# Sliding-window attention followed by an MLP: batching the softmax normalisation per head, and writing the attention loop as a software pipeline

## Chip, core and metric

The kernel runs on one core of a Trainium2 chip. The metric is the device time of one execution in microseconds (us). The kernel before took 407.39 us when it was first measured (median of 6 runs, 407.08 to 408.81).

## The reference

Four batches, eight heads, 768 positions, head size 64. A query sees the first 8 positions and the last 96 up to its own, with a distance bias that differs by head. The attention output, reshaped to 3072 x 512, goes through a two-layer MLP with a squared ReLU.

```python
scores = (1.0 / np.sqrt(D)) * np.matmul(q, k.transpose(0, 1, 3, 2))
keep = is_global | is_local                  # pos < 8, or 0 <= rel < 96
scores = np.where(keep, scores + bias, -1000000000.0)
a = np.exp(scores - np.max(scores, axis=-1, keepdims=True))
a = a / (np.sum(a, axis=-1, keepdims=True) + 1e-09)
x = np.matmul(a, v)                          # to (B*S, H*D)
h = x @ w_in                                 # 512 -> 2048
out = np.maximum(h, 0.0) ** 2 @ w_out        # 2048 -> 512
```

## The kernel before

Two heads form a pair; there are 16 pairs. For each pair, q and k of both heads are loaded, transposed on TensorE (12 transposes; the result lies in PSUM, as all matmul results of this kernel do) and copied by VectorE to SBUF, where its other tiles lie. Each head then has six tiles of 128 queries. A tile multiplies one to three blocks of keys with the queries (contraction over the 64 elements of a head), ScalarE takes the exponential, VectorE multiplies with a table of mask and bias, and TensorE multiplies with V. V has a 65th column of ones, so the row sum comes out beside the output, and VectorE divides by it.

```python
for b in range(B):
    for kp in range(H // 2):
        # ... load q_b, k_b; 12 transposes into qT_ps, kT_ps ...
        nc.vector.tensor_copy(qT2, qT_ps)
        nc.vector.tensor_copy(kT2, kT_ps)
        for hh in range(2):
            # ... load vS, then set its column of ones ...
            for t in range(N_ROW_TILES):
                # ... 1 to 3 score matmuls into sc_ps: lhsT = keys, rhs = queries, 64 rows each ...
                nc.scalar.activation(out=esc[:, :ncols], in_=sc_ps[:, :ncols], func=Act.Exp, scale=scale)
                nc.vector.tensor_mul(attnT[:, :ncols], esc[:, :ncols], expBT[h][cfg])
                out_ps = psum_out.tile([128, D + 1], FP32, tag="out_ps")
                # ... 1 to 3 output matmuls into out_ps ...
                nc.vector.reciprocal(rsum, out_ps[:, D : D + 1])
                nc.vector.tensor_scalar(out=x_sbuf[:, b * N_ROW_TILES + t, h, :], in0=out_ps[:, :D],
                                        scalar1=rsum, scalar2=None, op0=mybir.AluOpType.mult)
```

The program is not run in the order of this text: a scheduler places the instructions on each engine's queue when the kernel is built. The traces show the matmuls in the order that was built: the built order of this kernel changes 22 times per pair between scores and other matmuls, and so does its trace.

The softmax here doesn't subtract the row's maximum and nothing guards it: scores larger than these inputs give would overflow.

## Time and profile before

| Part of the span | Time |
|---|---|
| to the first score matmul (constants, MLP weights, first q and k) | 34.1 us |
| attention, 16 pairs, first score to last output | 180.7 us |
| rest: MLP | about 192 us |
| period of a head pair in the steady state | 11.35 us |

The first line is the busy time of each engine from the page; the second is one row of the windows view, 50 us of steady attention (busy us and instruction count of PE, of its weight loads PEld, of DVE, ACT and POOL, then granted TensorE clock, DMA share, GB/s); the third is the first long MLP piece in the chain of waits (start, duration).

```profile
PE 331.7 (81%) x2016; PEld 165.2 (41%) x2016; DVE 199.6 (49%) x712; ACT 161.2 (40%) x361; POOL 89.3 (22%) x158
...
50.00:100.00 50.00, 42.29 (x322) 24.72 (x320) 33.94 (x168) 22.28 (x53) 24.00 (x37) 1.00 0.84 54
...
216.62 4.85 PE hT_ps L290 x11
```

The clock of 1.00 in the second line is not a measurement: the trace has no clock record before 222.3 us, and the view prints 1.00 where there is none.

No engine is busy all the time in attention: TensorE (PE) has work for 42.3 of 50 us and VectorE (DVE) for 33.9. The next lines, the timeline of PE around the end of a pair, show where the rest goes (start, duration, what; in brackets the idle time and what ended it).

```profile
86.09 0.50 PE L218 MATMUL sc_ps<-qT,kT 64*128 64x128 bf16 x3
86.52 0.35 PE L239 MATMUL out_ps<-vS,attnT 128*128 128x65 bf16 x3
86.80 0.29 PE L218 MATMUL sc_ps<-qT,kT 64*128 64x128 bf16 x1
87.25 0.24 PE L239 MATMUL out_ps<-vS,attnT 128*128 128x65 bf16 x1 [0.17 <-DVE attnT L235]
87.42 0.39 PE L218 MATMUL sc_ps<-qT,kT 64*128 64x128 bf16 x2
87.94 0.29 PE L239 MATMUL out_ps<-vS,attnT 128*128 128x65 bf16 x2
88.40 0.70 PE L239 MATMUL out_ps<-vS,attnT 128*128 128x65 bf16 x6 [0.17 <-DVE attnT L235]
89.62 0.35 PE L239 MATMUL out_ps<-vS,attnT 128*128 128x65 bf16 x3 [0.52 <-DVE attnT L235]
90.49 0.35 PE L239 MATMUL out_ps<-vS,attnT 128*128 128x65 bf16 x3 [0.52 <-DVE attnT L235]
91.14 0.60 PE L218 MATMUL sc_ps<-qT,kT 64*128 64x128 bf16 x4 [0.31 <-DVE kT L189]
```

From 87.9 to 91.1 us TensorE has only output matmuls to do (14 of them), and all groups but the first show a wait for VectorE's mask multiply (attnT). It could not run the scores of the next pair, because the copy of the next keys (kT) had not been made. The timeline of DVE in the same stretch shows what VectorE did meanwhile:

```profile
88.61 0.28 DVE L250 TENSOR_SCALAR x_sbuf<-out_ps,rsum 128x64 bf16<-128x64 f32 x1
88.81 0.16 DVE L249 RECIPROCAL rsum<-out_ps 128x1 f32<-128x1 f32 x1
89.14 0.17 DVE L249 RECIPROCAL rsum<-out_ps 128x1 f32<-128x1 f32 x1 [0.17 <-PE out_ps L239]
89.22 0.34 DVE L235 TENSOR_TENSOR attnT<-esc,eT 128x384 bf16<-128x384 bf16 x1
89.48 0.47 DVE L250 TENSOR_SCALAR x_sbuf<-out_ps,rsum 128x64 bf16<-128x64 f32 x2
90.01 0.17 DVE L249 RECIPROCAL rsum<-out_ps 128x1 f32<-128x1 f32 x1
90.09 0.34 DVE L235 TENSOR_TENSOR attnT<-esc,eT 128x384 bf16<-128x384 bf16 x1
90.35 0.28 DVE L250 TENSOR_SCALAR x_sbuf<-out_ps,rsum 128x64 bf16<-128x64 f32 x1
90.54 0.55 DVE L189 COPY kT<-kT_ps 128x768 bf16<-128x768 bf16 x1
```

Mask multiplies stand between reciprocals and scalings, which wait for TensorE in turn, and the kT copy comes last. The two groups of small operations (busy us, mean ns; then idle before them), and the longest of the waits they are part of, from the groups and the waits view:

```profile
L249 DVE RECIPROCAL rsum<-out_ps 128x1 f32<-128x1 f32 x192 | 31.7, 165 | 52.0 <-PE out_ps L239 50.8
L250 DVE TENSOR_SCALAR x_sbuf<-out_ps,rsum 128x64 bf16<-128x64 f32 x192 | 49.4, 277 | 0.1
...
PEld L239 <- DVE attnT L235: 41.4, 97, 0.7
POOL vS L202 <- DMA vS<-in_v_dram: 44.4, 19, 4.1
```

Matmuls are pipelined, so their durations overlap, and the distance from one start to the next is what TensorE pays. Computed from the starts in the trace (60 to 200 us before, and 60 to 165 us after), these distances are, in ns:

```
from -> to             before (median)   after (mean)
output -> output             54               54
score -> score              106              102
transpose -> transpose       82               99
output -> score             176              177
score -> output             244              235
score -> transpose          243              231
transpose -> score          228              247
transpose -> output         106              107
```

Scores use 64 of the array's 128 rows, all others 128. A step between the two kinds takes 176 to 247 ns, a step within a kind or between output and transpose 53 to 107. The Trainium skill ("TensorEngine Tiling (Array Packing)", Key Properties) says that a change of tiling mode, as opposed to a change of tile, drains TensorE.

### The profile page before, as it was taken

Reading aid. Unit: us, or ns where it says so; the run is one execution under the profiler, and the core shown is the slowest. Engines: PE = TensorE matmul, PEld = TensorE weight load, DVE = VectorE, ACT = ScalarE, POOL = GpSimd, SP = SyncE. Lnnn points to the kernel's source line nnn. Section 1 sums busy time; section 2 is a strip of 40 time slices with the busy share of each in tenths; the row PEclk is TensorE's granted clock in tenths of the full one; section 3 lists DMA queues with packets and bytes.
Section 4 is the critical chain, followed back from the end, with each engine's and each line's share of the span. In section 5 each row is a group of like instructions: output and inputs, shape, how many; then the busy total and the mean of one; then the engine's idle time right before and its main releaser. Section 6 shows DMA issues by size and latency. Waiting matters only on the chain.

```text
span 407.0 us, 5774 instructions
## 1 busy us (share of the span) xinstructions
PE 331.7 (81%) x2016; PEld 165.2 (41%) x2016; DVE 199.6 (49%) x712; ACT 161.2 (40%) x361; POOL 89.3 (22%) x158
## 2 busy tenths in 40 slices
PE   0007888888988888888887998999999999999991
PEld 0005444444555444444452334434444434434430
DVE  0004776766666776776763444335335335345240
ACT  6403444444544444444451334235335235235232
POOL 9306634544543444531100000000000000000000
PEclk9999999999999999999999999999999999999998
DMA  3999997998677889763310002001101002002002
GB/s 52 201 190 107 79 58 50 58 60 57 44 48 50 52 55 60 50 38 21 22 10 0 2 0 86 19 0 53 52 0 70 35 1 91 15 2 103 0 2 103
DMA packets 81341, 20.30 MB, mean 50 GB/s; under 512 B 75680, under 2 KB 77728, under 8 KB 81312
## 3 DMA queue, kind: packets, MB, share of 16 engines
q0 software_dynamic: 77856, 13.64, 42.5%
q1 hardware_dynamic: 3456, 6.29, 4.1%
q8 instruction: 16, 0.26, 0.3%
q14 instruction: 13, 0.11, 0.1%
HBM read 27.26 MB, written 6.29 MB: 82 GB/s over the span
## 4 chain that ended last, share of the span: by engine, by line
PE 74%; DVE 14%; DMA 6%; issue 2%; POOL 2%; ACT 1%; DVEq 0%; POOLq 0%; ACTq 0%
PE hT_ps L290 21%; PE ps_out L303 20%; PE sc_ps L218 15%; PE out_ps L239 9%; DMA q_b<-in_q_dram 5%; DVE attnT L235 4%; PE kT_ps L181 4%; PE qT_ps L176 4%; DVE x_sbuf L250 3%; DVE rsum L249 3%; DVE kT L189 2%; DVE xT L284 2%; DVE h_sq L301 1%; ACT h_relu L299 1%; PE xTp L278 1%
## 5 line engine op out<-in xcount | busy, mean ns | idle before, releaser
L228 ACT ACTIVATE esc<-sc_ps 128x384 bf16<-128x384 f32 (+1 forms) x192 | 81.3, 438 | 117.7 <-PE sc_ps L218 80.6
L301 DVE TENSOR_TENSOR h_sq<-h_relu 128x512 bf16<-128x512 f32 x96 | 66.3, 692 | 108.7 <-ACT h_relu L299 108.7
L299 ACT ACTIVATE h_relu<-hT_ps 128x512 f32<-128x512 f32 x96 | 57.1, 600 | 109.2 <-PE hT_ps L290 108.9
L290 PE MATMUL hT_ps<-xT,w_in_sbuf 128*128 128x512 bf16 x384 | 92.5, 386 | 3.5 <-DVE xT L284 3.1
L303 PE MATMUL ps_out<-w_out_sbuf,h_sq 128*128 128x512 bf16 x384 | 91.0, 382 | 3.6 <-DVE h_sq L301 3.5
L218 PE MATMUL sc_ps<-qT,kT 64*128 64x128 bf16 x480 | 81.6, 301 | 5.8 <-DVE kT L189 5.8
L239 PE MATMUL out_ps<-vS,attnT 128*128 128x65 bf16 x480 | 62.8, 245 | 23.6 <-DVE attnT L235 21.3
L235 DVE TENSOR_TENSOR attnT<-esc,eT 128x384 bf16<-128x384 bf16 (+1 forms) x192 | 59.7, 311 | 4.3 <-ACT esc L228 1.0
L290 PEld LDWEIGHTS <-w_in_sbuf 128*128 128x128 bf16 x384 | 37.6, 99 | 51.2 <-issue 4.7
L249 DVE RECIPROCAL rsum<-out_ps 128x1 f32<-128x1 f32 x192 | 31.7, 165 | 52.0 <-PE out_ps L239 50.8
L239 PEld LDWEIGHTS <-attnT 128*128 128x128 bf16 x480 | 37.0, 124 | 47.7 <-DVE attnT L235 41.4
L303 PEld LDWEIGHTS <-h_sq 128*128 128x128 bf16 x384 | 31.9, 98 | 57.8 <-DVE h_sq L301 28.1
L218 PEld LDWEIGHTS <-kT 64*128 64x128 bf16 x480 | 40.0, 121 | 25.5 <-DVE kT L189 8.3
L250 DVE TENSOR_SCALAR x_sbuf<-out_ps,rsum 128x64 bf16<-128x64 f32 x192 | 49.4, 277 | 0.1
L176 PE MATMUL qT_ps<-ident,q_b 128*128 128x128 bf16 x96 | 18.5, 302 | 31.9 <-DMA q_b<-in_q_dram 31.6
L168 POOL DMA_DIRECT2D k_b<-in_k_dram x32 | 26.4, 824 | 34.7 <-PE out_ps L239 21.4
L198 POOL DMA_DIRECT2D vS<-in_v_dram x32 | 26.5, 830 | 16.0 <-POOL vS L202 7.3
L164 POOL DMA_DIRECT2D q_b<-in_q_dram x32 | 26.3, 824 | 16.7 <-PE out_ps L239 9.8
L176 PEld LDWEIGHTS <-q_b 128*128 128x128 bf16 x96 | 8.0, 120 | 39.2 <-issue 37.7
L188 DVE COPY qT<-qT_ps 128x768 bf16<-128x768 bf16 x16 | 8.6, 540 | 28.5 <-PE qT_ps L176 28.5
L181 PE MATMUL kT_ps<-ident,k_b 128*128 128x128 bf16 x96 | 22.1, 296 | 0.0
L314 ACT COPY out_tile<-ps_out 128x512 f32<-128x512 f32 x24 | 13.1, 590 | 12.8 <-PE ps_out L303 11.1
(42 smaller groups left out, 69.2 us busy)
## 6 DMA issues: line engine op xcount, KB each, us to landing
out_dram<-out_tile SPq DMA_DIRECT2D x24, 256.0 KB, 2.1
q_b<-in_q_dram POOLq DMA_DIRECT2D x32, 96.0 KB, 3.4
k_b<-in_k_dram POOLq DMA_DIRECT2D x32, 96.0 KB, 3.2
vS<-in_v_dram POOLq DMA_DIRECT2D x32, 96.0 KB, 3.2
w_in_sbuf<-in_moe_w_in_dram POOLq DMA_DIRECT2D x1, 2048.0 KB, 12.9
w_out_sbuf<-in_moe_w_out_dram POOLq DMA_DIRECT2D x1, 2048.0 KB, 23.1
```

What stands on the lines that cost most here:

```text
L176: nc.tensor.transpose(out=qT_ps[:, t * 128 : (t + 1) * 128], in_=q_b[:, t, :], identity=ident,)
L181: nc.tensor.transpose(out=kT_ps[:, t * 128 : (t + 1) * 128], in_=k_b[:, t, :], identity=ident,)
L218: nc.tensor.matmul(out=sc_ps[:, bi * 128 : (bi + 1) * 128], lhsT=kT[:, kb * 128 : (kb + 1) * 128], rhs=qT[:, r : r + 128], start=True, sto ...
L228: nc.scalar.activation(out=esc[:, :ncols], in_=sc_ps[:, :ncols], func=Act.Exp, scale=scale,)
L235: nc.vector.tensor_mul(attnT[:, :ncols], esc[:, :ncols], expBT[h][cfg])
L239: nc.tensor.matmul(out=out_ps, lhsT=attnT[:, 128 * bi : 128 * (bi + 1)], rhs=vS[:, kb, :], start=(bi == 0), stop=(bi == nblk - 1), skip_gr ...
L249: nc.vector.reciprocal(rsum, out_ps[:, D : D + 1])
L250: nc.vector.tensor_scalar(out=x_sbuf[:, b * N_ROW_TILES + t, h, :], in0=out_ps[:, :D], scalar1=rsum, scalar2=None, op0=mybir.AluOpType.mult,)
L290: nc.tensor.matmul(out=hT_ps, lhsT=w_in_sbuf[:, kt, c * 128 : (c + 1) * 128], rhs=xT[:, kt, :], start=(kt == 0), stop=(kt == KM - 1), skip ...
L299: nc.scalar.activation(h_relu, hT_ps, Act.Relu)
L301: nc.vector.tensor_mul(h_sq, h_relu, h_relu)
L303: nc.tensor.matmul(out=ps_out[:, sub, :], lhsT=h_sq[:, sub * 128 : (sub + 1) * 128], rhs=w_out_sbuf[:, c, :], start=(c == 0), stop=(c == C ...
```

## The change

It has two intents. The six tiles of a head share one PSUM bank, so one reciprocal and one multiply serve them all. And the loop becomes a software pipeline: scores are written two tiles ahead of outputs (LEAD), the next pair is transposed and copied from tile 5 of the current pair on, buffers grow, and VectorE's queue follows the program text and not the scheduler.

```diff
-    qkv_pool = ... bufs=2        work = ... bufs=3
+    qkv_pool = ... bufs=4        work = ... bufs=5
+    LEAD = 2
+    def load_pair(p): ...        # loads, transposes and copies, as before
+    def load_v(g):               # the column of ones is now set before the load of V
+    def front(i): ...            # scores, exponential, mask multiply of tile i
+    def back(i):
+        if t == 0:
+            outs[g] = psum_out.tile([128, N_ROW_TILES, D + 1], FP32, name="out_ps", tag="out_ps")
+        # ... output matmuls into out_ps[:, t, :] ...
+        if t == N_ROW_TILES - 1:
+            nc.vector.reciprocal(rsum, out_ps[:, :, D : D + 1])
+            nc.vector.tensor_mul(x_sbuf[:, b * N_ROW_TILES : (b + 1) * N_ROW_TILES, h, :],
+                                 out_ps[:, :, :D], rsum.to_broadcast([128, N_ROW_TILES, D]))
-                    nc.vector.reciprocal(rsum, out_ps[:, D : D + 1])
-                    nc.vector.tensor_scalar(out=x_sbuf[:, b * N_ROW_TILES + t, h, :], ...)
+    with tc.manual_schedule(engines={mybir.EngineType.DVE}):
+        load_pair(0)
+        for i in range(NT + LEAD):
+            if i < NT:
+                p, u = divmod(i, 2 * N_ROW_TILES)
+                if u == 5 and p + 1 < len(pairs):
+                    load_pair(p + 1)
+                front(i)
+            if i >= LEAD:
+                back(i - LEAD)
```

## The prediction

> **What bounds it now.** The windows view splits 407 us: about 32 us of constants and weight loads (the first transpose waits 31.6 us for q), attention to about 215 us, and the MLP (187 us from 220 us on, PE busy 174.7), where matmuls follow each other every 216 ns. The change touches attention only. There the chain of waits repeats every 11.35 us, per head pair (x6 score bursts at 79.80, 91.14, 102.50): 16 pairs = 181.6 us.
>
> Inside a pair the busy times are DVE about 7.9 us, ACT 5.1, POOL 5.2 (windows 50 to 150), and PE 9.5. Start-to-start distances in the timeline tell more: output matmuls follow each other in about 54 ns, scores in 81 to 107, transposes in 82, but going from output to score costs about 176 ns, from score to output 243, score to transpose 235, transpose to score 229. Scores use 64 rows of the array and the rest 128; the Trainium skill (TensorEngine Tiling, Key Properties) says that changing tiling mode drains TensorE[...]. Summing these over the 72 matmuls of a pair in the built order gives about 8.5 us without waits; so about 2.85 us per pair are waits. The timeline shows where: a run of 14 output matmuls waits for VectorE, whose queue holds 12 reciprocals and 12 scalings between the mask multiplies and ends with the kT/qT copies for which the next scores wait (87.2 to 91.1 us).
>
> **What the change does.** It removes 192 reciprocals (165 ns) and 192 scalings (277 ns), 81.1 us of DVE busy time, and adds 32 reciprocals of 128x6 (estimate 170 ns) and 32 multiplies of 128x384 from PSUM (estimate 610 ns, from 277 ns for 64 elements and 692 for 512 f32): 25 us. DVE falls from 199.6 to about 143 us in all, from 712 to about 392 instructions; per pair to about 5 us. The rest keeps its number and size. The new order issues transposes of the next pair early (runs of 6, 4 and 2), so the copies no longer stand in front of the scores; The ones-column is set before the V load, so POOL loses its 2.6 us waits for that landing. Mode changes per pair fall from 22 to 18: the same sum gives 7.9 us.
>
> **What is left.** DVE about 5, ACT 5, POOL 5.5 to 6 us per pair all lie under PE. DMA moves about 0.6 MB per pair; it reached 97 to 154 GB/s in some windows, 70 are needed. I expect small waits: the first mask multiplies of a head stand behind reciprocal and big multiply, which wait for the last output matmul (about 0.2 us twice), and bursts of eight scores run into the three score banks (about 0.1 us, several times). Period about 8.7 us, saving 2.65 x 16 = 42 us. MLP and start unchanged.
>
> **Time: 365 us**, 354 to 386 in 8 of 10 cases. Faster by over 2%: 0.96, within 2%: 0.03, slower: 0.01.
>
> **What would show it.** Right: period 8.3 to 9.2 us; DVE near 143 us; the big multiply near 610 ns; MLP still about 187 us; DVE waits of the output matmuls' weight loads (37 us) mostly gone. Wrong: period over 9.5, with PE waiting for ACT (score banks), for V or q loads (DMA), or for DVE, whose fixed order makes everything behind one reciprocal wait.
>
> **What could make it wrong:** PE's new order fits other durations than the chip's; loads at 70 GB/s may land too late; fixed DVE order may cost more than estimated.

## The result, and the profile after

The changed kernel takes 360.5 us (median of 8 runs, 359.49 to 360.84). The ratio to the kernel before is 0.8836 (95% interval 0.8825 to 0.8847). A ratio is the mean time of one kernel's fast runs over that of the other's fast runs of the same rounds, so it is not quite the ratio of the medians.

The same three lines as before, page, windows and chain:

```profile
PE 310.9 (87%) x2016; PEld 166.1 (46%) x2016; DVE 158.9 (44%) x392; ACT 157.0 (44%) x361; POOL 89.6 (25%) x158
...
50.00:100.00 50.00, 50.00 (x441) 34.67 (x441) 31.49 (x108) 29.14 (x73) 37.20 (x57) 1.00 1.43 92
...
168.81 4.28 PE hT_ps L308 x11
```

The MLP starts at 168.81 us and not at 216.62: 47.8 us are gained before it, and the rest is the same within 1 us (190.4 and 189.4 us from there to the end of the span). In attention TensorE is now busy for the whole 50 us; it does 441 matmuls in them and not 322. A stretch of its timeline, about half a pair:

```profile
85.01 0.51 PE L247 MATMUL out_ps<-vS,attnT 128*128 128x65 bf16 x6
85.45 0.50 PE L221 MATMUL sc_ps<-qT,kT 64*128 64x128 bf16 x3
85.88 0.34 PE L247 MATMUL out_ps<-vS,attnT 128*128 128x65 bf16 x3
86.16 0.28 PE L221 MATMUL sc_ps<-qT,kT 64*128 64x128 bf16 x1
86.37 0.40 PE L247 MATMUL out_ps<-vS,attnT 128*128 128x65 bf16 x4
86.71 0.39 PE L221 MATMUL sc_ps<-qT,kT 64*128 64x128 bf16 x2
87.03 0.29 PE L247 MATMUL out_ps<-vS,attnT 128*128 128x65 bf16 x2
87.26 1.11 PE L221 MATMUL sc_ps<-qT,kT 64*128 64x128 bf16 x8
```

No line has a wait in brackets. (The clock of 1.00 is no record: the trace of this kernel has none before 172.4 us.) What is left is the distances between starts: three scores and the step to the next output take 85.88 - 85.45 = 0.43 us, while three outputs and the step to the next score take 0.28. A pair takes 8.23 us, from one qT copy to the next.

The new groups of VectorE, its queue at the moment when the next pair is prepared, and the same waits of the whole execution:

```profile
L257 DVE RECIPROCAL rsum<-out_ps 128x6 f32<-128x6 f32 x32 | 6.3, 196 | 44.6 <-PE out_ps L247 44.6
L258 DVE TENSOR_TENSOR x_sbuf<-out_ps,rsum 128x384 bf16<-128x384 f32 x32 | 17.8, 557 | 1.1
...
87.46 0.88 DVE L234 TENSOR_TENSOR attnT<-esc,eT 128x384 bf16<-128x384 bf16 x3
88.27 0.55 DVE L187 COPY qT<-qT_ps 128x768 bf16<-128x768 bf16 x1
88.73 0.55 DVE L188 COPY kT<-kT_ps 128x768 bf16<-128x768 bf16 x1
...
PEld L247 <- DVE attnT L234: 9.4, 45, 0.7
POOL vS L196 <- PE out_ps L247: 26.8, 13, 4.0
```

The weight loads of the output matmuls wait 9.4 us for attnT in the whole execution and not 41.4, and mostly in pieces of about 0.2 us, in which TensorE still has matmuls in flight. POOL no longer waits for V to land before it can go on; it waits for a free V buffer, far ahead of its use.

### The profile page after: what moved, and what is told of

It is laid out like the page before. It is cut to its first block, busy times and chain, and to the rows that moved or that the text cites. A ratio compares the mean times of both kernels' runs of the same rounds, so it can differ in the third digit from the quotient of the medians.

```text
span 358.2 us, 5511 instructions
## 1 busy us (share of the span) xinstructions
PE 310.9 (87%) x2016; PEld 166.1 (46%) x2016; DVE 158.9 (44%) x392; ACT 157.0 (44%) x361; POOL 89.6 (25%) x158
## 4 chain that ended last, share of the span: by engine, by line
PE 84%; DMA 7%; DVE 4%; POOL 2%; ACT 2%; issue 1%; DVEq 0%; POOLq 0%; ACTq 0%
PE hT_ps L308 24%; PE ps_out L321 23%; PE sc_ps L221 19%; PE out_ps L247 11%; DMA w_out_sbuf<-in_moe_w_out_dram 6%; PE qT_ps L179 3%; PE kT_ps L182 3%; DVE xT L302 2%; DVE h_sq L319 1%; ACT h_relu L317 1%; PE xTp L296 1%; DMA out_dram<-out_tile 1%; ACT out_tile L332 0%; POOL q_b L168 0%; POOL k_b L172 0%
## 5 line engine op out<-in xcount | busy, mean ns | idle before, releaser
L230 ACT ACTIVATE esc<-sc_ps 128x384 bf16<-128x384 f32 (+1 forms) x192 | 77.1, 437 | 74.2 <-PE sc_ps L221 51.6
L221 PE MATMUL sc_ps<-qT,kT 64*128 64x128 bf16 x480 | 77.9, 301 | 1.4 <-DVE kT L188 1.0
L247 PE MATMUL out_ps<-vS,attnT 128*128 128x65 bf16 x480 | 53.8, 244 | 0.5 <-DVE attnT L234 0.5
L234 DVE TENSOR_TENSOR attnT<-esc,eT 128x384 bf16<-128x384 bf16 (+1 forms) x192 | 49.6, 316 | 3.8 <-PE out_ps L247 2.0
L221 PEld LDWEIGHTS <-kT 64*128 64x128 bf16 x480 | 42.2, 124 | 18.1 <-issue 3.8
L247 PEld LDWEIGHTS <-attnT 128*128 128x128 bf16 x480 | 34.0, 125 | 20.0 <-DVE attnT L234 9.4
L179 PE MATMUL qT_ps<-ident,q_b 128*128 128x128 bf16 x96 | 14.7, 309 | 31.2 <-POOL vS L196 31.2
L257 DVE RECIPROCAL rsum<-out_ps 128x6 f32<-128x6 f32 x32 | 6.3, 196 | 44.6 <-PE out_ps L247 44.6
L179 PEld LDWEIGHTS <-q_b 128*128 128x128 bf16 x96 | 9.2, 136 | 34.3 <-issue 33.8
L258 DVE TENSOR_TENSOR x_sbuf<-out_ps,rsum 128x384 bf16<-128x384 f32 x32 | 17.8, 557 | 1.1
L182 PE MATMUL kT_ps<-ident,k_b 128*128 128x128 bf16 x96 | 16.9, 307 | 0.0
```

The source lines that it names most:

```text
L179: nc.tensor.transpose(out=qT_ps[:, t * 128 : (t + 1) * 128], in_=q_b[:, t, :], identity=ident)
L182: nc.tensor.transpose(out=kT_ps[:, t * 128 : (t + 1) * 128], in_=k_b[:, t, :], identity=ident)
L221: nc.tensor.matmul(out=sc_ps[:, bi * 128 : (bi + 1) * 128], lhsT=kT[:, kb * 128 : (kb + 1) * 128], rhs=qT[:, r : r + 128], start=True, sto ...
L247: nc.tensor.matmul(out=out_ps[:, t, :], lhsT=attnT[:, 128 * bi : 128 * (bi + 1)], rhs=vSs[g][:, kb, :], start=(bi == 0), stop=(bi == len(k ...
```

## The experiments

The prediction left four questions: which part of the change took the waits away, what the fixed VectorE order is worth, whether the step between 64 and 128 rows is a real cost of the array, and what would come next. For each kernel the order of TensorE's instructions is known once it is built. The sum of start-to-start distances given below is the changed kernel's mean distances (the right column of the table above) added up over the built order, over ten pairs in the middle. It is an estimate of the pair's time without waits; for the changed kernel itself it must come out near the period, as its distances are the changed kernel's own. Buffers are those of q, k and v, then those of the attention tiles. All twelve runs gave correct results.

| Kernel | Normalisation | Lead | Next pair prepared | Buffers | VectorE order | Sum of distances, us | Period, us | Median, us |
|---|---|---|---|---|---|---|---|---|
| before | per tile | 0 | in its own pair | 2, 3 | free | 8.79 | 11.35 | 407.7 |
| e6 | per tile | 0 | in its own pair | 4, 5 | free | 8.55 | 11.88 | 415.9 |
| e11 | per tile | 0 | early | 2, 3 | free | 8.18 | about 10.5 | 397.4 |
| e9 | per tile | 2 | in its own pair | 4, 5 | free | 8.04 | 10.28 | 391.8 |
| e10 | per tile | 0 | early | 4, 5 | free | 8.21 | 9.53 | 380.8 |
| e5 | per tile | 2 | early | 4, 5 | free | 8.72 | 8.58 | 366.2 |
| e2 | per tile | 2 | early | 4, 5 | fixed | 9.00 | 8.83 | 371.3 |
| e1 | per head | 0 | in its own pair | 2, 3 | free | 8.27 | 8.26 | 363.1 |
| after | per head | 2 | early | 4, 5 | fixed | 8.21 | 8.23 | 360.5 |
| e3 | per head | 2 | early | 4, 5 | free | 7.95 | 7.91 | 354.4 |
| e7 | per head | 4 | early | 4, 5 | fixed | 7.44 | 7.67 | 352.3 |

Where period and sum agree, no more waits are left than in the changed kernel. e5 and e2 take less than their sums, by 0.14 and 0.17 us: that is the error of the sum.

### Half of the change at a time: e1 and e2

e1 is the kernel before with the batched normalisation alone:

```diff
+                out_ps = psum_out.tile([128, N_ROW_TILES, D + 1], FP32, tag="out_ps")
                 for t in range(N_ROW_TILES):
-                    out_ps = psum_out.tile([128, D + 1], FP32, tag="out_ps")
...
-                            out=out_ps,
+                            out=out_ps[:, t, :],
...
+                rsum = scalar_pool.tile([128, N_ROW_TILES, 1], FP32, tag="rsum")
+                nc.vector.reciprocal(rsum, out_ps[:, :, D : D + 1])      # after the loop over t
+                nc.vector.tensor_mul(x_sbuf[...six tiles..., h, :], out_ps[:, :, :D], rsum.to_broadcast(...))
```

> The kernel before with one edit: six row tiles of a head share one output bank, and one reciprocal and one multiply serve them. Loop order, buffers and the scheduler's freedom stay. Theory A (the waits came from the 24 small operations in VectorE's queue): the order built from it has 18 changes between 64-row and 128-row matmuls per pair and 8.27 us of start-to-start distances, so the period is 8.3 to 8.7 us and the time 360 to 368 us. Rival B (the gain comes from writing scores two tiles ahead of outputs and from more buffers): most waits stay, period over 10 us, time over 387 us.

It took 363.11 us, ratio 0.8909, with a period of 8.26 us. So the batching alone is worth 44.6 of the 47.2 us, with the old loop, buffers and free scheduling. It does one more thing than to remove small operations: three banks now hold the outputs of 18 tiles and not of 3. In the kernel before the output matmuls waited for attnT and hardly for a tile to be freed (their weight loads waited 0.4 us for x_sbuf in the whole execution), but no run tests this apart.

e2 is the reverse: the changed kernel with a reciprocal and a scaling per tile.

```diff
-        if t == N_ROW_TILES - 1:
-            nc.vector.reciprocal(rsum, out_ps[:, :, D : D + 1])
-            nc.vector.tensor_mul(...)
+        nc.vector.reciprocal(rsum, out_ps[:, D : D + 1])
+        nc.vector.tensor_scalar(out=x_sbuf[:, b * N_ROW_TILES + t, h, :], in0=out_ps[:, :D],
+                                scalar1=rsum, scalar2=None, op0=mybir.AluOpType.mult)
```

> The changed kernel with the old normalisation of each row tile (384 small VectorE operations) put back; lead, buffers, fixed VectorE order stay. The order has 24 changes of row count per pair, 9.0 us of start-to-start distances. Theory A: VectorE needs about 8 us per pair again and its queue waits for output matmuls, so waits are added: period 10 us or more, time over 385 us. Rival B: the lead hides them, period 9.0 to 9.4 us, time 373 to 380 us.

It took 371.34 us (ratio 0.9114), period 8.83 us: a little less than the rival's 373 to 380 us, and not what my theory expected. The window of 50 to 100 us in e2:

```profile
50.00:100.00 50.00, 50.00 (x409) 30.43 (x409) 47.03 (x218) 30.12 (x70) 34.65 (x54) 1.00 1.32 85
```

VectorE is busy for 47 of 50 us with the small operations and TensorE still never idles. So each half of the change takes nearly all waits away by itself, and the two do not add up: once TensorE has no waits, the period is what its order of matmuls costs.

### The fixed VectorE order: e3 and e5

e3 and e5 are the changed kernel and e2 with one edit:

```diff
-    with tc.manual_schedule(engines={mybir.EngineType.DVE}):
+    if True:
```

> The changed kernel without the fixed VectorE order (the scheduler places VectorE too). The order built has 16 changes per pair and 7.95 us of start-to-start distances. If the array is the bound and there are no waits, the period is 8.0 us and the time 357 us, so the fixed order is worth nothing or a little less than nothing; if the fixed order is what removes the waits, the period is over 9 us and the time over 372 us.

> As e2 (old normalisation, lead and buffers of the change), but without the fixed VectorE order. 22 changes per pair, 8.72 us of start-to-start distances. If lead or buffers hid VectorE's queue in e2, the period is 8.6 to 8.9 us and the time 366 to 371 us; if the fixed order did it, waits come back: period over 9.5 us, time over 382 us.

e3 took 354.39 us (0.8701, period 7.91 us), e5 366.19 us (0.8985, period 8.58 us). Freed, both are 5 to 6 us faster. TensorE hardly waits in any of the four kernels; what differs is the order that the scheduler builds for TensorE around VectorE's. e3 has 16 changes between 64 and 128 rows per pair where the changed kernel has 18, and e5 has 22 where e2 has 24.

### Which part of the pipelining hides the small operations: e6, e9, e10, e11

All four keep the normalisation per tile and the free order. e6 is the kernel before with the new buffer counts. e9 is e5 with `load_pair(p)` moved to the start of its own pair; e10 is e5 with `LEAD = 0`; e11 is e10 with the old buffer counts.

```diff
 e6, against the kernel before
-    name="qkv", bufs=2 ... name="work", bufs=3
+    name="qkv", bufs=4 ... name="work", bufs=5
 e9, against e5
-                if u == 5 and p + 1 < len(pairs):
-                    load_pair(p + 1)
+                if u == 0 and p > 0:
+                    load_pair(p)
 e10, against e5
-    LEAD = 2
+    LEAD = 0
 e11, against e10
-    name="qkv", bufs=4 ... name="work", bufs=5
+    name="qkv", bufs=2 ... name="work", bufs=3
```

> The kernel before with the change's buffer counts alone (4 and 5 in place of 2 and 3). The order built has 20 changes per pair and 8.55 us of start-to-start distances. If buffers alone let the scheduler hide VectorE's queue, the period is 8.5 to 9 us and the time 363 to 372 us; if the lead is needed, waits stay: period over 10 us, time over 390 us.

> As e5 (old normalisation, lead of two, new buffers, free scheduling), but the next pair's q and k are transposed and copied at the start of their own pair, not at tile 5 of the pair before. The order built has a run of 21 output matmuls per pair and only 16 changes, 8.04 us of start-to-start distances. If the early preparation is what took the waits away, they are back: period 10.5 to 12 us, time 395 to 418 us. If the lead did it, the period is 8.0 to 8.3 us, time 356 to 362 us.

> As e5 but with a lead of 0 and the early preparation kept. 18 changes per pair, 8.21 us of start-to-start distances. If the early preparation suffices, period 8.2 to 8.6 us, time 359 to 366 us; if the lead is needed, over 9.5 us and over 380 us.

> As e10 with the old buffer counts (2 and 3): of the change only the early preparation is left (and the ones column set before the V load). 18 changes per pair, 8.18 us. If the moment of the preparation alone is the cause of the waits before, period 8.2 to 8.8 us, time 358 to 369 us. If buffers are needed too, V or q loads or the attn tiles hold TensorE: over 9.2 us, over 375 us.

e6 took 415.93 us, 2% more than the kernel before (ratio 1.0206, 95% interval 1.0191 to 1.0222: clear of noise, but at the 2% line the verdict is "unclear"), although its sum of distances is smaller. With more attention tiles to fill, the built order puts 18 output matmuls and not 14 in a row at the end of a pair, all of which wait for VectorE. That the longer run is the reason was not tested apart.

e9 took 391.82, e10 380.84 and e11 397.39 us (ratios 0.9613, 0.9336 and 0.9749). e9 fell between the alternatives that I had written down, and e10 and e11 came out as those where more parts are needed: no single part does it. With small operations, early preparation (with the column of ones set first) is worth 10 us (e11), new buffers on top of it 17 more (e10), and the lead 15 more (e5). Lead and buffers without early preparation are worth 16 (e9), and buffers alone cost 8 (e6). The order of e9 has a run of 21 outputs before the next pair's scores, and the waits of the output matmuls for VectorE are back, in another form: from 60 to 150 us their weight loads wait 21.5 us for x_sbuf, the scaling that frees one of the three output tiles. In e11 the output matmuls waited 10.5 us for V to land in the same stretch, so there the old buffer counts are part of it.

### The number of row changes: e7

The lead is 4 in place of 2 in the changed kernel, which lengthens the runs of one kind.

```diff
-    LEAD = 2
+    LEAD = 4
```

> The changed kernel with a lead of 4 tiles in place of 2. The order built has 12 changes of row count per pair in place of 18, 7.44 us of start-to-start distances in place of 8.21. If the number of changes sets the period, it is 7.4 to 7.6 us and the time 347 to 351 us. If lookahead matters for waits alone, which are gone already, nothing moves: 8.2 us, 360 us. If longer score runs meet the three score banks, waits appear and the time is over 352 us.

It took 352.29 us (0.8642), period 7.67 us: 8.2 us faster than the changed kernel, and 1.3 us over the range that I gave. A longer lead helps although no waits were left, because the order has 12 changes per pair and not 18. About 0.2 us per pair are still lost, to what the third expectation named: of each run of 12 scores the tenth, which begins a fourth tile, starts 249 ns after the ninth, 50 ns after ScalarE's exponential of an earlier tile ends. There are three score banks, so it waits for one of them. Twice per pair at 143 ns over the usual 106, that is 0.29 us.

### The price of a row change: e4 and e12

e4 is the changed kernel with the keys of each head in a tile of 128 rows, of which the other head's 64 are zero. The scores are the same, but contract over 128 rows as all other matmuls do.

```diff
+    kz = []                                   # two buffers for each of the two heads, zeroed once
+    for i in range(2):
+        kz.append([])
+        for hh in range(2):
+            z = consts.tile([128, S], BF16, name=f"kz{i}{hh}", tag=f"kz{i}{hh}")
+            nc.vector.memset(z[(1 - hh) * D : (2 - hh) * D, :], 0.0)
+            kz[i].append(z)
...
-        kT2 = tqk.tile([128, S], BF16, name="kT2", tag="kT2")
+        kT2 = kz[p % 2]
...
-        nc.vector.tensor_copy(kT2, kT_ps)
+        for hh in range(2):
+            rows = slice(hh * D, (hh + 1) * D)
+            nc.vector.tensor_copy(kT2[hh][rows, :], kT_ps[rows, :])
...
-        qT = qT2[p0 : p0 + D, :]
-        kT = kT2[p0 : p0 + D, :]
+        qT, kT2 = qk[g // 2]
+        kT = kT2[h % 2]
```

> The changed kernel with keys of each head in a 128-row tile whose other 64 rows are zero, so that score matmuls contract over 128 rows like all others; one more VectorE copy per pair. Theory (the 176 and 243 ns between scores and others are the price of changing the row tiling): these distances fall to 54 to 110 ns, the matmuls of a pair need 4.5 to 6 us, ScalarE, VectorE or POOL become the bound, period 5.5 to 6.8 us, time 318 to 338 us. Rival (they are a latency of semaphores, banks or weights that has nothing to do with row count): period 8.2 to 8.4 us, time 360 to 363 us.

It took 328.38 us, ratio 0.8062, and the period fell from 8.23 to 6.18 us in the steady state. Computed from the starts in the trace (45 to 95 us), the median distance from score to output fell from 243 to 55 ns, from score to score from 106 to 55, from score to transpose from 231 to 56; from output to score it fell from 176 to 128 only, though the shortest was 29. Two lines of PE's timeline, the window of 50 to 100 us, then a stretch of 3.3 us at half the granted clock with three lines of PE's timeline in it:

```profile
94.40 0.33 PE L228 MATMUL sc_ps<-qT,kz 128*128 128x128 bf16 x3
94.57 0.26 PE L254 MATMUL out_ps<-vS,attnT 128*128 128x65 bf16 x3
...
50.00:100.00 50.00, 40.99 (x562) 31.65 (x562) 46.19 (x151) 34.07 (x94) 47.42 (x73) 0.97 1.76 113
...
61.70:65.00 3.30, 3.15 (x35) 2.99 (x36) 2.42 (x7) 2.73 (x7) 3.30 (x6) 0.50 1.92 124
...
63.63 0.51 PE L228 MATMUL sc_ps<-qT,kz 128*128 128x128 bf16 x3
63.94 0.37 PE L254 MATMUL out_ps<-vS,attnT 128*128 128x65 bf16 x3
64.12 0.51 PE L228 MATMUL sc_ps<-qT,kz 128*128 128x128 bf16 x3
```

Three scores and the step to the next output take 94.57 - 94.40 = 0.17 us, where they took 0.43. But not all of this is the row count. From output to output the median fell from 53 to 36 ns and from transpose to transpose from 106 to 56, although these matmuls have 128 rows in both kernels. The rate of TensorE had changed too. Two lines of the kernel before, from its chain of waits, show at what rate it came out of attention:

```profile
216.62 4.85 PE hT_ps L290 x11
...
223.67 1.73 PE hT_ps L290 x8
```

The first MLP matmuls start 427 ns apart, and from the first clock record on (222.3 us, at 1.00) the same matmuls start 216 ns apart. All eleven kernels without padding show these two distances, with the change at their first clock record; none has a record in attention. So attention ran at half rate in all of them, with the distances that the table above gives. e4 has records from 37.7 us on, at 1.00 but for one stretch at 0.50 (61.6 to 65.0 us). The stretches at 0.50 in e4, e8 and e12 (both below) show what padding does when the rate does not change. Median distances in ns, computed from the starts:

```
from -> to             64 rows, half rate   padded, clock 0.50   padded, clock 1.00
                       (changed kernel)     (e4, e8, e12)        (e4)
output -> score             176                  55                  128
score -> output             243                 107                   55
score -> transpose          231                 107                   55
transpose -> score          247                 107                  159
score -> score              106                 106                   55
output -> output             53                  55                   36
transpose -> transpose      106                 107                   55
```

In the lines at 0.50 three scores and the step to the next output take 63.94 - 63.63 = 0.31 us, against 0.43 without padding. At the same rate a step between scores and others takes 121 to 140 ns less once all have 128 rows, and a step within a kind is unchanged. So the price of the steps belongs to the row count, and the rival is out for them. That agrees with what the page says of a change of mode; a drain itself is not seen in a trace. The shorter distances inside the runs are the rate's. Taken off the changed kernel's 18 changes, this price brings its sum from 8.2 to about 5.9 us per pair (an estimate from this table), which is enough for the period of 6.18. Why the clock was granted in full once the keys were padded, and what that alone is worth in e4, was not tested. TensorE now idles 9 of 50 us, and VectorE (46.2 of 50) and POOL (47.4, it runs ahead here) are the busiest.

e12 is the same padding in the kernel before, where it takes the place of the kT2 tile.

> The kernel before with the padded keys of e4 and nothing else. The padding takes 2 to 2.5 us of matmul distances out of a pair, as in e4, and adds a VectorE copy in front of the next scores. If the kernel before waits at the pair boundary for VectorE, most of that is not gained: period 10 to 11.5 us, time 387 to 412 us. If the array sets its pace, the period falls like in e4 by 2 us: 9.3 us, 375 us.

It took 384.83 us (ratio 0.9441), a mean period of 9.84 us (attention over 16): neither branch. It doesn't tell cleanly what padding is worth there, because the granted TensorE clock changed to and fro. Two of its windows (the clock is the number before the last two):

```profile
60.00:80.00 20.00, 14.50 (x146) 11.49 (x144) 16.91 (x80) 9.43 (x24) 9.63 (x16) 0.66 0.86 55
80.00:100.00 20.00, 14.47 (x145) 11.59 (x146) 16.82 (x81) 9.52 (x24) 10.51 (x17) 0.66 0.94 61
```

The clock was 0.66 on average here, while the kernel before ran its attention at half rate. So a part of the 23 us may be the rate's, and what the padding is worth in the kernel before at one rate stays open.

### A version that beats both: e8

e8 joins the padding, the free order and a third thing: the MLP weights (4 MB in bf16) no longer go ahead of the first q and k, but in eight pieces between the pairs.

```diff
-    nc.gpsimd.dma_start(out=w_in_sbuf, in_=moe_w_in.rearrange("(km p) f -> p km f", p=128))
-    nc.gpsimd.dma_start(out=w_out_sbuf, in_=moe_w_out.rearrange("(kf p) f -> p kf f", p=128))
+    def load_weights(c): ...                 # a quarter of w_in (c < 4) or of w_out (c < 8)
...
                     load_pair(p + 1)
+                if u == 8 and p >= 3:
+                    load_weights(p - 3)
```

> A version meant to beat both: the changed kernel with the keys padded to 128 rows (e4), without the fixed VectorE order (e3), and with the MLP weights loaded in eight pieces between the pairs, not ahead of the first q and k. The first transpose then waits for 96 KB and not for 4 MB: it should start near 12 us in place of 31, saving 15 to 20 us; the period stays near e4's 6.3 us or falls to 6. Time 300 to 316 us. If the weight pieces delay the q, k and v loads, the period rises and the time is over 316 us.

It took 313.57 us (310.61 to 314.98), ratio 0.7682, inside the range expected. The first score matmul starts at 13.5 us and not at 33.8, but attention from there takes 104.3 us where e4's takes 100.7. In the steady state many pairs take 5.81 us, but some take 6.1 to 9.2, and this wait of e8 (45 to 105 us) tells of one reason:

```profile
PE out_ps L264 <- DMA vS<-in_v_dram: 12.1, 7, 3.2
```

Output matmuls waited 12.1 us for V there, which e4 did for 0.2 us in the same stretch. The weight pieces go through the same DMA queue as q, k and v, and the loads of V took 4.5 us in the median to land, against 3.2 in the kernel before. Two stretches at a clock of 0.50 (6.8 and 3.4 us) fall among the long pairs too; the two reasons were not separated. A better place for the pieces was not searched for.

## Why the prediction was right

The time of 360.5 us lies in the range of 354 to 386, 4.5 us below the 365 predicted. Point by point:

- **The bound before** was right: about 2.6 to 2.8 us per pair of waits at the end of a pair, on top of 8.5 to 8.8 us of matmul distances. The prediction named both the small operations in VectorE's queue and the late copies for the next pair, but did not ask what each is worth. Without the small operations the waits go (e1). With them, they go too if lead, early preparation and buffers come together (e5); early preparation alone does not do it (e11, about 10.5 us).
- **The size of the saving** was 47.2 us where 42 were predicted. The period is 8.23 us and not 8.7. Two terms were off in opposite directions and in part cancelled, which is luck. The sum of distances was put at 7.9 us and is 8.2: the prediction took transposes at 82 ns, and in the new order they average 99, which over nine such steps is half of the difference; the rest was not traced. The small waits were put at about 0.8 us, and nearly all of them are absent: the timeline shows no idle time in 50 us. One of the kinds named is there, once per pair: a score starts 236 ns after the one before it, 50 ns after one of ScalarE's exponentials ends (the score banks are three), about 0.13 us over the usual distance. The waits for VectorE were costed as if each late operation delayed TensorE, but scores are written two tiles ahead of outputs, and TensorE has them to do meanwhile.
- **VectorE's busy time** was mis-sized: 158.9 us and not 143. It fell by 40.7 us where 56 were predicted. The two groups removed add up to 81.1 us, but neighbouring operations on VectorE overlap in the trace (a reciprocal starts at 90.01 for 0.17 us, the next multiply at 90.09), and the engine's busy time counts such a stretch once: without the two groups the busy time in the trace before would be 48.8 us less, not 81.1. A sum of groups overstates what removing them takes off. It did not matter for the time, because VectorE was no longer the bound.
- **The new multiply** takes 557 ns, estimated 610. The Trainium skill ("VectorE: DVE Perf Modes", The TRN2 errata) has (N + 151) / 0.96 ns for an fp32 tensor_tensor add; for N = 384 that is an estimate of 557, as measured, though this is a multiply that reads one operand from PSUM and writes bf16.
- **The row changes** fell from 22 to 18 as the built order said, and e4 and e7 show that they are a large part of the period once the waits are gone. The prediction read their size from distances at half rate without knowing it. That did no harm, because both kernels ran at that rate. The fixed VectorE order, named as a risk because of waits, costs 6 us (e3); the two more row changes per pair in its order are the main difference in the sums (8.21 and 7.95 us).
- **MLP and start** were unchanged, to 1 us.

## What to carry to other kernels

Before costing the waits that a change removes, add up the distances between matmul starts in the order that will be built: that sum is where the time lands when the waits are gone, and here it was right to 0.3 us per pair. Two measures against the same wait don't add up, so test each alone; batching six small VectorE operations into one did here about what lead, early preparation and buffers together did. When TensorE is busy without a gap, look at how often it changes between shapes: padding a 64-row contraction to 128 rows with zeros took another 9% off, together with the rise of TensorE's rate that came with it. And a clock of 1.00 in a view is worth a check against the distances between matmuls: here it stood for a stage without a record, which ran at half rate.

## What the Trainium skill lacked or had wrong

- "TensorEngine Tiling (Array Packing)", Key Properties, says that a change of tiling mode drains TensorE, but not what it costs. Here a step between 64-row and 128-row matmuls took 176 to 247 ns from start to start; with all rows alike, at the same half rate, it took 55 to 107 (the stretches of e4, e8 and e12 at a clock of 0.50), so the change costs 121 to 140.
- The same page (When to Use Tiling) recommends row tiling for a contraction of 64. Where such matmuls alternate with 128-row ones and only one row tile is used at a time, as here, the padded form was faster: 328.4 against 360.5 us, a higher rate of TensorE included. The page doesn't weigh the two.
- "TensorE: Matmul & The Clock Gate" (Why this matters for your kernels) advises against idle gaps of over about 3 us, which bring the clock back to half. That does not explain what is seen here. The changed kernel's TensorE has no idle gap from 50 to 100 us, yet its attention ran at half rate: transposes started 106 ns apart in attention and 56 in the MLP. In e12 the granted clock switched between 1.00 and 0.50, mostly every 3 to 7 us, while the longest gap between TensorE's busy spans in attention was 1.6 us. The page also tells of a kernel whose clock swings because of short idle times; whether e12 is such a case was not settled, and what kept the unpadded kernels at half rate was not either.
- "VectorE: DVE Perf Modes", The TRN2 errata, gives 120 + N cycles for an operation that reads PSUM. For the 128x384 multiply that is an estimate of 525 ns; the trace has 557, which is the page's other formula, given for fp32 tensor_tensor.
